# Another order for the first nine tiles of a fused attention and feed-forward kernel

## The chip, the cores and the metric

The kernel runs on one core of one Trainium2 chip. A core has TensorE (PE; its weight loads are PEld), VectorE (DVE), ScalarE (ACT), GpSimd (POOL) and the queues that issue transfers, SP's above all. Each engine works off its own instructions in the order in which they stand and waits on semaphores for the others. The metric is the device time of one execution in microseconds (us). Before the change it is 477.7 us, the median of three runs (477.04 to 478.3).

## The reference: what is computed

Chunked attention, then a feed-forward block with a SoLU and a layer norm:

```
scores = (q_c @ k_c^T) / 8          # batch 8, heads 8, 9 chunks of 64, head size 64
attn   = exp(scores - max); attn /= sum(attn) + 1e-9
x      = attn @ v_c                 # put together as 4608 tokens x 512
h      = x @ w_in                   # 512 x 1024
solu   = h * softmax(h)
ln     = (solu - mean) / sqrt(var + 1e-6) * g_ln
out    = ln @ w_out                 # 1024 x 512
```

q, k and v are float32. The weights reach the kernel as float64, as pairs of 32-bit words; the matrix products run as three products of two float32r halves each (high by high, high by low, low by high), so each weight matrix must first be cut into a high and a low part.

## The kernel before, in words

The 4608 tokens are 36 tiles of 128 tokens; a tile holds two chunks of each of the eight heads. From tile 5 on a loop runs one tile after another in a fixed pattern. Ahead of the loop stands a start in which four things run together: the weights are loaded and converted, attention is computed for tiles 0 to 7, the feed-forward products of tiles 0 to 4 are made, and the loads for the loop are begun. The order of that start is written out by hand as a string of words, START (lines 18 to 31). A word names a step and its tile or unit; where a word stands several times, each place issues the next piece of that step. Every engine keeps the order in which the words reach it. MOVED (lines 34 to 37) names the pieces that run on another engine than usual.

The steps that matter here:

- `n:i` two loads of q and k of tile i as they lie (256 KB each, one slot for even and one for odd tiles); `v:i` the load of v (256 KB); `P:x` a load of one unit of weights, 1 MB (unit 0 in two halves; units 0 to 3 are `w_in`, 4 to 7 `w_out`); `g` the load of g_ln; `q` some loads of the loop's q and k (`q_st`, `k_st`, 72 KB each). SP issues them all.
- A unit's conversion: `c:x` limits the upper words (line 188, tile `w_a`), then ACT scales them in place; `b:x` turns the lower words into bits (line 198, tile `w_b`); `C:x` joins both on DVE; `t:x` writes the high part on ACT; `d:x` the low part on DVE.
- Attention of tile i: `N` four PE transposes of q or of k and a copy out of PSUM to `qT` or `kT`; `S` scores on PE; `A` maximum and subtraction on DVE, then exponential on ACT; `B` sum, reciprocal and multiplication on DVE (the multiplication has both inputs in SBUF); `T` transposes on PE and four copies on ACT; `V` values on PE, then `x_h` on ACT and `x_l` on DVE.
- Feed-forward: `M:i` 24 products into `ph` on PE (tile 0 in four parts, part m with unit m); `X` maximum on DVE and exponential on ACT; `Y` a multiplication on DVE and an affine step on ACT or POOL; `R` the variance on ACT and POOL; `z` transposes of tiles 0 and 1 on PE with `z_h` on ACT and `z_l` on DVE; `Z` the same for tiles 2 and 3 by a DVE transpose and 16 transfers; `F` eight products into `po` on PE; `o` the scaling and the store on ACT; `w:n` n products of the identity that compute nothing.

`ph` has one buffer, except that tile 1 has one of its own: products of tile 2 and later wait until the multiplication of `Y` of the tile before in that buffer has read it. `w_a` and `w_b` have two buffers each. All transfers of SP and ACT share eight semaphores in turn, so each also waits for the landing of the one eight places ahead.

Every recorded operation has line 54 in the profile, that of the helper which keeps the order; rows are told apart by tiles.

Of the kernel before, what the change touches and what calls it, by code (L numbers as in the profile page):

```python
# [15 lines left out]


START = """
n:0 w:3 N:0:0 N:0:0 w:1 N:0:1 N:0:1 g w:1 S:0 A:0 G P:0 P:0 n:1 A:0 c:0 c:0 w:3 N:1:0 N:1:0 w:1
N:1:1 b:0 N:1:1 G P:1 w:1 S:1 B:0 v:0 C:0 A:1 t:0 T:0 T:0 c:1 c:1 w:4 V:0 V:0 P:2 b:1 c:2 n:2  # L20
d:0 P:3 A:1 n:3 w:6 N:2:0 w:1 N:2:1 C:1 V:0 B:1 t:1 c:2 T:1 N:2:0 b:2 N:2:1 T:1 d:1 S:2 n:4
M:0 M:0 C:2 t:2 c:3 c:3 v:1 A:2 A:2 b:3 d:2 C:3 N:3:0 N:3:1 N:3:1 M:0 N:3:0 S:3 N:4:0 B:2 N:4:1
t:3 N:4:0 A:3 P:5 d:3 c:5 N:4:1 A:3 T:2 T:2 S:4 V:1 M:0 P:4 n:5 B:3 T:3 V:1 V:1 M:1 X:0 X:0 T:3
A:4 A:4 b:4 v:2 N:5:1 c:4 n:6 P:7 c:5 N:5:0 c:4 Y:0 Y:0 n:7 N:5:1 V:2 b:5 v:3 B:4 N:5:0 V:2 b:7
C:4 z:0:1 P:6 v:5 N:6:0 X:1 v:4 C:5 N:6:0 S:5 Q:2 q:8 t:4 V:2 d:4 N:6:1 N:6:1 X:1 t:5 A:5 Y:1
M:2 z:0:1 z:0:1 X:2 A:5 R:0 z:0:0 z:0:0 q:8 N:7:1 q:8 c:6 S:6 Y:1 V:3 X:2 T:4 T:4 z:0:0 d:5 F
V:3 Y:2 Y:2 N:7:0 A:6 c:6 c:7 V:3 b:6 B:5 C:6 n:8 N:7:0 M:3 R:1 c:7 q:8 N:7:1 C:7 T:5 z:1:0 t:6
T:5 S:7 t:7 d:6 X:3 X:3 d:7 V:4 V:4 Y:3 Y:3 R:2 z:1:1 A:6 F F A:7 V:4 z:1:0 z:1:0 v:6 Z:2 A:7
M:4 F B:7 Z:3 o:0 V:5 z:1:1 z:1:1 B:6 F F v:7 X:4 N:8:0 X:4 U:6 U:7 V:5 Y:4 V:5 K:9 Y:4 N:8:0
R:4 R:3 N:8:1 N:8:1 o:1  # L30
"""


MOVED = """
N:0:0=dve N:8:0=dve N:8:1=dve Y:0=pool Y:1=pool Y:3=pool b:7=pool c:0=pool c:1=pool c:2=pool
c:3=pool c:4=pool c:5=pool c:6=pool c:7=pool
"""


# [23 lines left out]
def chunk_attention_then_solu_ffn(  # L63
# [12 lines left out]
    B, H, S, D = q.shape  # L76
    DM, FF = H * D, g_ln.shape[0]
    P = 128
# [3 lines left out]
    G = S // 32  # L82
# [24 lines left out]
    def po():  # L107
# [8 lines left out]
    moved = dict(w.split("=") for w in MOVED.split())  # L116
    order.on = False
    pe, dve, act, pool, sync = (
        order.engine(e)
        for e in (nc.tensor, nc.vector, nc.scalar, nc.gpsimd, nc.sync)  # L120
    )
# [89 lines left out]
    def paired(w):  # L211

        return w.rearrange("p (a x b) -> p a x b", x=2, b=P)
# [14 lines left out]
    def unit_low(x):  # L228
        kind, m = UNITS[x]
        a, top = scaled.pop(x), tops.pop(x)  # L230
        if kind == "in":
            dve.tensor_tensor(
                out=paired(wi_l[:, m, :]),
                in0=a.rearrange("p h (a b x) -> p (h a) x b", b=P, x=2),
                in1=top.bitcast(F32), op=ALU.subtract,
            )
            return
        for y in range(2):
            dve.scalar_tensor_tensor(
                out=wo_l[:, 2 * m + y, :], in0=a[:, y],  # L240
                scalar=g_sb[:, 2 * m + y:2 * m + y + 1], in1=top[:, y].bitcast(F32),
                op0=ALU.mult, op1=ALU.subtract,
            )


    QT, KT, V, QS, KS = {}, {}, {}, {}, {}
# [129 lines left out]
    def softmax_b(i):  # L376
        e = st[i, "e"]
        ssum = small.tile([P, H], F32, name="s_sum")
        dve.tensor_reduce(out=ssum, in_=ES[i % 2], axis=AX.X, op=ALU.add)
        rinv = small.tile([P, H], F32, name="s_rinv")  # L380
        dve.reciprocal(out=rinv, in_=ssum)
        a = st[i, "e"] = work.tile([P, H, CH], F32, name="s_e") if i < PE_TURNED else e
        dve.tensor_tensor(
            out=a, in0=e, in1=rinv.unsqueeze(2).to_broadcast([P, H, CH]), op=ALU.mult,
        )

# [330 lines left out]
    def warm(n):  # L717
# [8 lines left out]
        "P": load_pair, "n": load_natural,  # L726
        "v": load_v, "g": load_g, "Q": load_batch, "q": load_some,
        "G": scale_g, "N": turn_natural, "S": scores, "A": start_softmax, "B": softmax_b,
        "T": attn_transpose, "U": attn_turn, "V": start_values, "c": unit_scale,
        "b": unit_bits, "C": unit_join, "t": unit_high, "d": unit_low, "M": ffn_in, "X": solu_a, "Y": solu_b,  # L730
        "R": variance, "Z": z_turn, "z": z_half, "F": product, "o": store,
        "K": turn, "w": warm,
# [17 lines left out]
    for i in range(first, NT):  # L750
# [9 lines left out]
        if not odd:  # L760

            if i + 3 < NT:
                softmax_e(i + 3)
                softmax_b(i + 3)
                attn_turn(i + 3)
            if i + 1 < NT:
                x_high(i + 1)
# [27 lines left out]
        if odd:  # L795
            if i + 1 < NT:
                x_low(i + 1)
            if i + 3 < NT:
                softmax_b(i + 3)
                attn_turn(i + 3)  # L800
        else:
            for m in (i + 4, i + 5):
                if m < NT:
                    turn(m)
# [45 lines left out]
```

## Time and profile before

| what | us |
|---|---|
| median of three runs | 477.7 |
| the profiled execution | 477.95 |
| its span | 476.2 |
| PE busy | 465.6 (98%) |
| DVE busy | 374.3 (79%) |
| ACT busy | 256.5 (54%) |
| POOL busy | 147.7 (31%) |

A row of the timeline has the start, the duration, engine, line, operation, output and inputs, shape and count; in brackets stands how long the engine was idle before it and what ended that. A row of the windows has, for each engine, busy time and the number of instructions, then the granted TensorE clock, the share of the transfer engines and their rate. The granted clock is 1.00 throughout.

### The profile page before, as it was taken

To read this page: it belongs to the slowest core of one execution; us is meant where nothing else is said; L and a number is where in the kernel's file an instruction comes from. 1 tells how busy PE (TensorE), PEld (TensorE's weight loads), DVE (VectorE), ACT (ScalarE), POOL (GpSimd) and SP (SyncE) were. 2 spreads that over 40 slices of the span, in tenths; PEclk is the share of its full clock that TensorE was granted. 3 is DMA by queue.
4 is the path that set the end of the run, shared out by engine and by line. 5 is a ranking of instruction groups with operands and counts; after the bars stand their busy time and mean duration, and the time that the engine had idled before them with its cause. 6 is when DMAs were issued, how large, how long until landed. Compare 5 with 4: busy or idle time off the path is not lost.

```text
span 476.2 us, 11114 instructions
## 1 busy us (share of the span) xinstructions
PE 465.6 (98%) x4212; PEld 382.6 (80%) x4212; DVE 374.3 (79%) x520; ACT 256.5 (54%) x423; POOL 147.7 (31%) x298
## 2 busy tenths in 40 slices
PE   7899998999999999999999999999999999999997
PEld 5677786888888888888888888888888888888876
DVE  3999997798869887878787878797979797954441
ACT  2879982646444645454545455454555554545552
POOL 2212725150505050505050505032414141423330
PEclk9999999999999999999999999999999999999999
DMA  8999979758886878696358596949743435343221
GB/s 221 308 288 220 202 134 199 166 154 154 200 144 162 158 175 166 164 168 154 88 138 159 136 185 144 182 110 188 156 115 97 126 90 135 85 116 104 74 60 73
DMA packets 192924, 72.57 MB, mean 152 GB/s; under 512 B 177188, under 2 KB 177960, under 8 KB 191976
## 3 DMA queue, kind: packets, MB, share of 16 engines
q1 hardware_dynamic: 185768, 58.23, 55.4%
q0 software_dynamic: 6528, 12.86, 10.4%
q8 instruction: 33, 0.54, 0.5%
q10 hardware_dynamic: 576, 0.79, 0.5%
q14 instruction: 19, 0.16, 0.1%
HBM read 36.70 MB, written 9.44 MB: 97 GB/s over the span
## 4 chain that ended last, share of the span: by engine, by line
PE 85%; DMA 6%; SPq 3%; DVE 3%; ACT 1%; issue 1%; ACTq 0%
PE po L54 38%; PE ph L54 38%; PE tp L54 5%; PE sx L54 4%; SPq L54 3%; DMA nat<-in_k_dram 2%; DMA nat<-in_q_dram 2%; DMA z_t<-z_b 1%; DMA k_st<-in_k_dram 1%; DVE h_nmax L54 0%; DVE w_a L54 0%; DVE wo_l L54 0%; ACT attn_t L54 0%; ACT z L54 0%; ACT z_h L54 0%
## 5 line engine op out<-in xcount | busy, mean ns | idle before, releaser
L54 PE MATMUL ph<-wi_l,x_h 128*128 128x512 f32 x288 | 112.9, 392 | 1.9 <-DVE z L54 1.8
L54 PE MATMUL po<-wo_l,z_h 128*128 128x512 f32 (+1 forms) x288 | 113.3, 393 | 0.1
L54 ACT ACTIVATE z<-ph,h_nmax 128x1024 f32<-128x1024 f32 x36 | 40.2, 1117 | 134.6 <-DVE h_nmax L54 134.6
L54 PE MATMUL ph<-wi_h,x_h 128*128 128x512 f32 x288 | 112.1, 389 | 0.0
L54 PE MATMUL po<-wo_h,z_l 128*128 128x512 f32 (+1 forms) x288 | 111.9, 389 | 0.0
L54 PE MATMUL po<-wo_h,z_h 128*128 128x512 f32 (+1 forms) x288 | 111.4, 387 | 0.0
L54 POOL DMA_DIRECT2D z_t<-z_b x144 | 71.7, 505 | 28.7 <-DVE z_b L54 24.5
L54 PE MATMUL ph<-wi_h,x_l 128*128 128x512 f32 x288 | 78.1, 390 | 0.0
L54 POOL TENSOR_TENSOR u<-ssq,eps 128x1 f32<-128x1 f32 x36 | 7.1, 198 | 212.1 <-ACT sq L54 211.9
L54 DVE TENSOR_REDUCE h_nmax<-ph 128x1 f32<-128x1024 f32 x36 | 44.0, 1221 | 30.2 <-PE ph L54 30.2
L54 PEld LDWEIGHTS ph<-wi_l,x_h 128*128 128x128 f32 x288 | 54.1, 188 | 13.8 <-ACT x_h L54 2.2
L54 PEld LDWEIGHTS po<-wo_h,z_l 128*128 128x128 f32 x288 | 54.1, 188 | 12.1 <-DVE z_l L54 1.0
L54 PEld LDWEIGHTS po<-wo_l,z_h 128*128 128x128 f32 x288 | 54.1, 188 | 11.9 <-ACT z_h L54 0.5
L54 PEld LDWEIGHTS ph<-wi_h,x_l 128*128 128x128 f32 x288 | 53.9, 188 | 11.6 <-DVE x_l L54 0.4
L54 PEld LDWEIGHTS ph<-wi_h,x_h 128*128 128x128 f32 x288 | 54.1, 188 | 11.0
L54 PEld LDWEIGHTS po<-wo_h,z_h 128*128 128x128 f32 x288 | 54.1, 188 | 10.5
L54 DVE TENSOR_TENSOR z_l<-z_t,z_h 128x1024 fp32r<-128x1024 f32 (+1 forms) x37 | 42.0, 1136 | 25.3 <-ACT z_h L54 23.9
L54 DVE SCALAR_TENSOR_TENSOR z<-ph,z 128x1024 f32<-128x1024 f32 x36 | 43.9, 1219 | 13.3 <-ACT z L54 13.2
L54 ACT ACTIVATE z<-z,z_sum 128x1024 f32<-128x1024 f32 x33 | 38.1, 1154 | 23.0 <-DVE z L54 22.4
L54 DVE STREAM_TRANSPOSE z_b<-z 128x1024 f32<-128x1024 f32 x34 | 41.2, 1211 | 3.8 <-ACT z L54 3.1
L54 ACT CAST z_h<-z_t 128x1024 fp32r<-128x1024 f32 (+1 forms) x37 | 35.9, 970 | 8.6 <-PE po L54 6.5
L54 ACT ACTIVATE o_sb<-po,r 128x512 f32<-128x512 f32 (+1 forms) x36 | 24.2, 673 | 24.9 <-POOL r L54 18.6
(76 smaller groups left out, 598.6 us busy)
## 6 DMA issues: line engine op xcount, KB each, us to landing
out_dram<-o_sb SPq DMA_DIRECT2D x33, 256.0 KB, 2.5
v_sb<-in_v_dram SPq DMA_DIRECT2D x32, 256.0 KB, 4.4
z_t<-z_b POOLq DMA_DIRECT2D x128, 64.0 KB, 2.8
z_t<-z_b SPq DMA_DIRECT2D x128, 64.0 KB, 2.9
q_st<-in_q_dram SPq DMA_DIRECT2D x96, 72.0 KB, 3.1
k_st<-in_k_dram SPq DMA_DIRECT2D x96, 72.0 KB, 3.1
w_raw<-in_moe_w_out_dram SPq DMA_DIRECT2D x4, 1024.0 KB, 7.4
attn_t<-a_b POOLq DMA_DIRECT2D x60, 64.0 KB, 3.8
```

The lines of the kernel that those rows point to most:

```text
L54: ins = make(*args, **kwargs)
```

## The change

START is another sequence of the same words, and MOVED names another set of pieces. The words before and after are the same, but that two `w:3` have become `w:2` (19 of the empty products in place of 21). Two steps, `d` and `B`, get the possibility to run on POOL, which MOVED does not use.

```diff
 START = """
-n:0 w:3 N:0:0 N:0:0 w:1 N:0:1 N:0:1 g w:1 S:0 A:0 G P:0 P:0 n:1 A:0 c:0 c:0 w:3 N:1:0 N:1:0 w:1
+P:1 c:1 c:1 n:0 n:1 w:6 N:0:0 P:0 P:0 b:1 w:1 N:0:1 N:0:0 C:1 N:0:1 t:1 w:1 S:0 n:2 N:1:0 A:0
...
 MOVED = """
-N:0:0=dve N:8:0=dve N:8:1=dve Y:0=pool Y:1=pool Y:3=pool b:7=pool c:0=pool c:1=pool c:2=pool
-c:3=pool c:4=pool c:5=pool c:6=pool c:7=pool
+N:0:0=dve N:8:0=dve Y:2=pool Y:3=pool Y:4=pool b:2=pool b:5=pool c:0=pool c:2=pool c:3=pool
+c:4=pool c:5=pool c:6=pool c:7=pool
 """
...
         if kind == "in":
-            dve.tensor_tensor(
+            (pool if f"d:{x}" in moved else dve).tensor_tensor(
...
         a = st[i, "e"] = work.tile([P, H, CH], F32, name="s_e") if i < PE_TURNED else e
-        dve.tensor_tensor(
+        (pool if f"B:{i}" in moved else dve).tensor_tensor(
```

So c:1 and b:7 go from POOL to DVE, b:2 and b:5 from DVE to POOL, one copy of tile 8 from DVE to ACT, and of the affine steps Y:0 and Y:1 go from POOL to ACT, Y:2 and Y:4 from ACT to POOL.

**SP's queue at the start.** `nat` are the q and k of a tile, `w_raw` a unit of weights. Before:

```order
L54 DMA nat_95<-in_q_dram 128x8x64
L54 DMA nat_95<-in_k_dram 128x8x64
L54 DMA g_in_103<-in_moe_g_ln_dram 4x256
L54 DMA w_raw_151<-in_moe_w_in_dram 128x1024 x2
L54 DMA nat_95<-in_q_dram 128x8x64
L54 DMA nat_95<-in_k_dram 128x8x64
L54 DMA w_raw_183<-in_moe_w_in_dram 128x2048
L54 DMA v_sb_209<-in_v_dram 128x8x64
L54 DMA w_raw_252<-in_moe_w_in_dram 128x2048
```

With the change:

```order
L54 DMA w_raw_104<-in_moe_w_in_dram 128x2048
L54 DMA nat_95<-in_q_dram 128x8x64
L54 DMA nat_95<-in_k_dram 128x8x64
L54 DMA nat_95<-in_q_dram 128x8x64
L54 DMA nat_95<-in_k_dram 128x8x64
L54 DMA w_raw_127<-in_moe_w_in_dram 128x1024 x2
L54 DMA nat_95<-in_q_dram 128x8x64
L54 DMA nat_95<-in_k_dram 128x8x64
L54 DMA w_raw_201<-in_moe_w_in_dram 128x2048
L54 DMA g_in_103<-in_moe_g_ln_dram 4x256
L54 DMA v_sb_230<-in_v_dram 128x8x64
L54 DMA nat_95<-in_q_dram 128x8x64
```

Unit 1 now comes first, ahead of q and k of tiles 0 and 1; unit 0 follows those; v of tile 0 comes behind unit 2, and q and k of tile 3, which stood behind unit 3, stand ahead of it.

**PE ahead of tile 0's products**, from the values of tile 0 (`sx<-attn_t,v_sb`) to the first product into `ph` with weights. Before:

```order
L54 MATMUL sx_96<-attn_t_94,v_sb_209 64x64 x16
L54 MATMUL ph_266<-ident_79 128x256 x6
L54 MATMUL tp_275<-ident_79,nat_95 128x128 x4
L54 MATMUL ph_280<-ident_79 128x256
L54 MATMUL tp_282<-ident_79,nat_95 128x128 x4
L54 MATMUL tp_297<-ident_79,s_e_293 128x128 x4
L54 MATMUL sx_96<-kT_274,qT_273 64x64 x16
L54 MATMUL ph_331<-wi_l_91,x_h_249 128x512
```

With the change:

```order
L54 MATMUL sx_96<-attn_t_94,v_sb_230 64x64 x16
L54 MATMUL tp_314<-ident_79,nat_95 128x128 x4
L54 MATMUL ph_329<-ident_79 128x256
L54 MATMUL tp_331<-ident_79,nat_95 128x128 x4
L54 MATMUL tp_339<-ident_79,s_e_324 128x128 x4
L54 MATMUL sx_96<-kT_313,qT_312 64x64 x16
L54 MATMUL ph_376<-wi_l_91,x_h_309 128x512
```

The rows read alike, but the transposes of q and k and the scores are those of tile 2 before and of tile 3 now: one tile more is turned and scored ahead of tile 0's products.

**DVE around POOL's b:5.** `w_b_522` is written by b:5 on POOL, `w_a_454` belongs to unit 4 and `w_a_476` to unit 5. With the change DVE has:

```order
L54 TENSOR_SCALAR w_b_568<-w_raw_411 128x1024
L54 SCALAR_TENSOR_TENSOR z_570,z_sum_574<-ph_376,z_570 128x1024
L54 SCALAR_TENSOR_TENSOR w_a_454<-w_a_454,w_b_568 128x1024
L54 TENSOR_REDUCE s_nmax_577<-sx_96 128x8
L54 TENSOR_TENSOR e1_98<-sx_96,s_nmax_577 128x8x64
L54 TENSOR_TENSOR x_l_566<-sx_96,x_h_565 128x512
L54 TENSOR_REDUCE h_nmax_618<-ph_580 128x1
L54 TENSOR_TENSOR z_l_102<-tp_611,z_h_101 128x512
L54 SCALAR_TENSOR_TENSOR w_a_476<-w_a_476,w_b_522 128x1024
```

and POOL has:

```order
L54 TENSOR_SCALAR w_a_203<-w_raw_127 128x1024
L54 TENSOR_SCALAR w_a_261<-w_raw_201 128x1024
L54 TENSOR_SCALAR w_b_326<-w_raw_201 128x1024
L54 TENSOR_SCALAR w_a_383<-w_raw_273 128x1024
L54 TENSOR_SCALAR w_a_454<-w_raw_411 128x1024
L54 TENSOR_SCALAR w_a_476<-w_raw_435 128x1024
L54 TENSOR_SCALAR w_b_522<-w_raw_435 128x1024
```

In this order POOL does c:0, c:2, b:2, c:3, c:4, c:5, b:5. Before it did c:0, c:1, c:2, c:3, c:5, c:4, then an affine step and b:7. The multiplication of Y:0 and C:4 stand ahead of five DVE instructions that read PSUM, and C:5, which needs b:5, behind them.

More of the change, by code (lines that the diff above doesn't have):

```diff
@@ L18 @@
 START = """
-n:0 w:3 N:0:0 N:0:0 w:1 N:0:1 N:0:1 g w:1 S:0 A:0 G P:0 P:0 n:1 A:0 c:0 c:0 w:3 N:1:0 N:1:0 w:1
[L20 to L30, printed above, removed]
+P:1 c:1 c:1 n:0 n:1 w:6 N:0:0 P:0 P:0 b:1 w:1 N:0:1 N:0:0 C:1 N:0:1 t:1 w:1 S:0 n:2 N:1:0 A:0
@@ new lines @@
+N:1:0 N:1:1 N:1:1 w:2 S:1 d:1 A:0 P:2 c:0 c:0 A:1 w:2 N:2:0 N:2:0 w:1 N:2:1 b:0 g v:0 B:0 N:2:1
+w:1 S:2 C:0 n:3 A:1 c:2 T:0 t:0 T:0 P:3 n:4 A:2 G d:0 w:4 V:0 c:2 A:2 V:0 N:3:0 N:3:0 B:1 b:2 G
+w:1 N:3:1 v:1 N:3:1 T:1 V:0 T:1 S:3 B:2 C:2 A:3 t:2 M:0 c:3 M:0 n:5 c:3 v:2 N:4:0 b:3 N:4:0
+N:4:1 P:4 V:1 d:2 T:2 P:5 A:3 N:4:1 C:3 n:6 B:3 M:0 c:4 P:6 S:4 v:3 c:5 t:3 d:3 N:5:0 T:2 A:4
+V:1 V:1 N:5:1 N:5:1 N:5:0 M:0 P:7 A:4 X:0 B:4 b:5 T:3 T:3 S:5 V:2 V:2 b:4 X:0 c:4 Y:0 C:4 A:5
+M:1 Y:0 n:7 c:5 t:4 z:0:0 z:0:0 V:2 X:1 X:1 N:6:1 N:6:1 A:5 v:5 z:0:0 C:5 b:6 R:0 Q:2 q:8 d:4
@@ L31 @@
+M:2 Y:1 N:6:0 X:2 t:5 z:0:1 N:6:0 V:3 z:0:1 X:2 c:6 c:7 S:6 d:5 z:0:1 T:4 T:4 Y:2 V:3 v:4 F
+N:7:0 Y:2 Y:1 c:6 A:6 N:7:1 V:3 N:7:1 N:7:0 M:3 c:7 B:5 R:2 b:7 C:6 V:4 t:6 C:7 t:7 S:7 n:8 d:6
+z:1:0 T:5 d:7 F Z:2 T:5 X:3 V:4 V:4 F z:1:0 q:8 X:3 z:1:1 z:1:0 q:8 A:6 z:1:1 Y:3 V:5 V:5 A:7
+q:8 Y:3 v:6 z:1:1 F A:7 R:3 o:0 v:7 M:4 B:6 B:7 Z:3 X:4 U:6 U:7 F F X:4 R:1 Y:4 Y:4 N:8:1 V:5
+N:8:1 R:4 N:8:0 o:1 N:8:0 K:9
 """
 MOVED = """
-N:0:0=dve N:8:0=dve N:8:1=dve Y:0=pool Y:1=pool Y:3=pool b:7=pool c:0=pool c:1=pool c:2=pool
```

## The prediction

> **What bounds the kernel now.** I read the page first, then the busy time by stages, then PE's timeline, and followed PE's waits to what ended them.
>
> ```profile
> PE 465.6 (98%) x4212; PEld 382.6 (80%) x4212; DVE 374.3 (79%) x520; ACT 256.5 (54%) x423; POOL 147.7 (31%) x298
> PE   7899998999999999999999999999999999999997
> DVE  3999997798869887878787878797979797954441
> ```
>
> PE has hardly a gap. But part of it is empty products and waiting that counts as busy, so the stages say more:
>
> ```profile
> 0.00:23.36 23.36, 19.15 (x204) 14.58 (x205) 14.69 (x21) 13.14 (x20) 5.15 (x13) 1.00 0.93 264
> 23.36:34.21 10.85, 10.74 (x150) 8.40 (x145) 10.57 (x16) 9.20 (x16) 1.28 (x2) 1.00 1.17 290
> 34.21:82.15 47.94, 45.19 (x428) 36.20 (x426) 43.54 (x63) 34.20 (x64) 20.71 (x24) 1.00 0.92 191
> 82.15:200.00 117.85, 117.73 (x1104) 97.21 (x1105) 99.93 (x141) 62.33 (x102) 38.12 (x84) 1.00 0.77 163
> 200.00:400.00 200.00, 200.00 (x1822) 165.83 (x1821) 167.87 (x237) 104.19 (x168) 60.91 (x132) 1.00 0.63 142
> ```
>
> (columns: window, its length, then PE, PEld, DVE, ACT, POOL, clock, transfers' share, GB/s.) From 82.15 us on PE idles 0.12 us in 318: whatever PE gains by then reaches the end whole. 23.36 is where tile 0's first product starts, 34.21 that of tile 1, 82.15 that of tile 5, with which the loop begins. DVE is busy for 10.57 of 10.85 us and 43.54 of 47.94 in these stages, so it is a second chain as long as PE's. The transfers are full (0.93, 1.17) until 34 us: they set when the start can begin.
>
> ```profile
> 20.39 0.66 PE L54 MATMUL tp<-ident,nat 128*128 128x128 f32 x4 [0.65 <-DMA nat<-in_q_dram]
> 22.74 0.69 PE L54 MATMUL sx<-kT,qT 64*64 64x64 f32 x32 [0.24 <-ACT kT L54]
> 23.36 0.50 PE L54 MATMUL ph<-wi_l,x_h 128*128 128x512 f32 x1
> 40.55 1.06 PE L54 MATMUL tp<-ident,nat 128*128 128x128 f32 x8 [0.62 <-DMA nat<-in_k_dram]
> 41.55 0.69 PE L54 MATMUL sx<-attn_t,v_sb 64*64 64x64 f32 x32
> 82.15 0.47 PE L54 MATMUL ph<-wi_l,x_h 128*128 128x512 f32 x1 [1.84 <-DVE z L54]
> ```
>
> Tile 0's products start behind tile 2's scores, whose q landed at 20.39. Of the 2.75 us in which PE idles from 34.21 to 82.15 (47.94 - 45.19), 0.62 and 1.84 stand here. The longer one begins on ACT:
>
> ```profile
> 75.03 0.41 ACTq L630 DMA_DIRECT2D out_dram<-o_sb  x1
> 75.49 0.59 ACT L54 CAST z_h<-tp 128x512 fp32r<-128x512 f32 x1 [5.97 <-DMA k_st<-in_k_dram]
> 76.11 0.69 DVE L54 TENSOR_TENSOR z_l<-tp,z_h 128x512 fp32r<-128x512 f32 x1 [2.80 <-ACT z_h L54]
> 78.28 1.22 DVE L54 TENSOR_REDUCE h_nmax<-ph 128x1 f32<-128x1024 f32 x1
> 80.77 1.22 DVE L54 SCALAR_TENSOR_TENSOR z<-ph,z 128x1024 f32<-128x1024 f32 x1
> ```
>
> The store of tile 0 stood in ACT's queue for a `k_st` load of SP; behind it waited tile 1's `z_h`, behind that DVE, so tile 4's maximum came at 78.28 and its multiplication freed `ph` only at 82.
>
> **The change part by part.** Time is counted at the start of tile 5's products, 82.15 now; by then both kernels have done the same PE work.
>
> *When tile 0's products start.* POOL's c steps show when weights land:
>
> ```profile
> 9.60 1.62 POOL L54 TENSOR_SCALAR w_a<-w_raw 128x1024 f32<-128x1024 f32 x1 [8.17 <-DMA w_raw<-in_moe_w_in_dram]
> 14.17 1.14 POOL L54 TENSOR_SCALAR w_a<-w_raw 128x1024 f32<-128x1024 f32 x1 [2.95 <-DMA w_raw<-in_moe_w_in_dram]
> 17.98 1.54 POOL L54 TENSOR_SCALAR w_a<-w_raw 128x1024 f32<-128x1024 f32 x1 [2.68 <-DMA w_raw<-in_moe_w_in_dram]
> 24.14 1.13 POOL L54 TENSOR_SCALAR w_a<-w_raw 128x1024 f32<-128x1024 f32 x1 [4.62 <-DMA w_raw<-in_moe_w_in_dram]
> ```
>
> By 14.17 units 0 and 1 and q and k of tiles 0 and 1 are there, 3 MB; the change loads the same 3 MB first, so unit 0, now last of them, lands at 14.2 in place of 9.6, and unit 1 much earlier. From 14.17 to 24.14 came 2.75 MB, 3.63 us per MB (3.05 and 4.1 in its two pieces). The change needs unit 2 after 1.5 MB more: 19.6; v of tile 0 at 20.5; k of tile 3 after 2.25 MB: 22.3 (21.0 to 23.4). From there the copy to `kT` is held by ACT's queue, priced by these starts:
>
> ```profile
> 22.10 0.59 ACT L54 COPY kT<-tp 128x512 f32<-128x512 f32 x1 [0.43 <-PE tp L54]
> 22.58 1.54 ACT L54 COPY attn_t<-tp 64x256 f32<-64x256 f32 x4
> 24.14 1.14 ACT L54 CAST wi_h<-w_a 128x1024 fp32r<-128x1024 f32 x1
> 25.30 1.06 ACT L54 ACTIVATE w_a<-w_a 128x1024 f32<-128x1024 f32 x1
> 26.27 0.61 ACT L54 ACTIVATE e<-e 128x512 f32<-128x512 f32 x1
> ```
>
> A copy takes 0.48, four attention copies 1.56, a weight cast 1.16, a scaling 0.97, an exponential about 0.55. Unit 0 at 14.2, b:0 on DVE (0.6) and c:0 on POOL (1.1) one after the other: ACT can scale it at 16.1. Then follow scaling, five copies or `x_h`, two exponentials, one cast, the four copies and unit 2's scaling: 0.97 + 2.4 + 1.1 + 1.16 + 1.56 + 0.97 = 8.2, with 0.3 of short waits 24.6. Scores (0.62 by 22.74 to 23.36) and 0.2 of handing over: **25.4**, 2.0 later than 23.36. Bounds: 24.4 with the fastest loads, 27.9 with the slowest and c:0 held.
>
> *Work moved ahead of it.* Tile 3's eight transposes (40.55 to 41.55: 1.0) and its scores (0.62) leave what follows: -1.6.
>
> *The waits that go.* q and k of tile 6, which PE waited for at 40.55, now stand behind 1 MB less of weights; and tile 0's store comes after tile 3's variance on ACT, when tile 4's products are still running, so a late `k_st` no longer holds a `z_h` that PE needs. SP starts `q_st` earlier (units 4 to 7 and tiles 4 to 7 come in a row); the rows that price it, before, are
>
> ```profile
> 51.20 12.81 SPq L54 DMA_DIRECT2D q_st<-in_q_dram  x16
> 70.13 6.02 SPq L54 DMA_DIRECT2D k_st<-in_k_dram  x8
> ```
>
> 0.8 and 0.75 us per load. From about 47 the 27 loads and four others before the store's predecessor make 70; ACT is there at 70 and needs to be on with tile 4's exponential only at about 75: five us of cover, without which PE waits what exceeds it. -2.5 together; bounds 0 and -2.75.
>
> *Steps on other engines.*
>
> ```profile
> L54 ACT ACTIVATE z<-z,z_sum 128x1024 f32<-128x1024 f32 x33 | 38.1, 1154 | 23.0 <-DVE z L54 22.4
> L54 POOL TENSOR_SCALAR z<-z,z_sum 128x1024 f32<-128x1024 f32 x3 | 3.8, 1250 | 8.3 <-DVE z L54 8.2
> ```
>
> The four affine steps that change places are a draw: 1.15 us on ACT, 1.25 on POOL. c:1 on DVE costs what b:2 gives there, and b:7 what b:5 gives; tile 8's copy leaves DVE. DVE's load stays the same. But on POOL:
>
> ```profile
> 17.28 1.23 DVE L54 SCALAR_TENSOR_TENSOR w_a<-w_a,w_b 128x1024 uint32<-128x1024 uint32 x1
> 36.65 1.10 POOL L54 TENSOR_SCALAR w_a<-w_raw 128x1024 f32<-128x1024 f32 x1 [1.47 <-DMA w_raw<-in_moe_w_out_dram]
> 36.82 1.48 DVE L54 TENSOR_SCALAR w_b<-w_raw 128x1024 uint32<-128x1024 uint32 x1
> 39.36 0.68 DVE L54 TENSOR_SCALAR w_b<-w_raw 128x1024 uint32<-128x1024 uint32 x1
> 47.60 3.73 POOL L54 TENSOR_SCALAR w_b<-w_raw 128x1024 uint32<-128x1024 uint32 x1 [6.57 <-DVE s_nmax L54]
> ```
>
> A b takes 0.68 on DVE and 3.73 on POOL, and the two engines hold one another: DVE's b at 36.82 ended at 38.30, 0.55 after POOL's c that had begun before it (37.75), and POOL's c at 17.98 took 1.54, not 1.13, because it had to let C at 17.28 end (18.51). So POOL waits for a DVE instruction with two SBUF inputs; that DVE waits so for POOL no row shows. Where b:7 stands now, DVE reads PSUM all along and loses nothing. b:2 (from 20.7) has B:1's multiplication in its way, which tile 1's transposes ahead of tile 3's scores need: between 0 and 2.7 us of DVE, which is 0 to 1.3 on tile 0's start (26.7 at worst) and up to 0.7 at its last part, since C:2 needs b:2 anyway. I take 0.4 and 0.2, nearer the lower end, since no row shows the whole. b:5 comes after c:5; unit 5 lands 3.5 MB after unit 3 (25.5), at 38.1 with 3.63 per MB, 39.1 with 3.85 (24.14 to 36.65 for 3.25 MB). b:5 then starts about 40, as C:4 does. Behind C:4 DVE has five instructions that read PSUM, four of 512 columns and one of 1024, priced by
>
> ```profile
> 33.76 0.69 DVE L54 TENSOR_TENSOR x_l<-sx,x_h 128x512 fp32r<-128x512 f32 x1
> 34.37 1.21 DVE L54 TENSOR_REDUCE h_nmax<-ph 128x1 f32<-128x1024 f32 x1
> ```
>
> 4 x 0.69 + 1.21, less 0.08 of overlap at each of four seams (33.76 + 0.69 - 34.37): 3.65 us, just b:5's length. I take 0; bounds 0 and 3.7.
>
> *Sum.* +2.0 + 0.4 - 1.6 - 2.5 + 0.2 = -1.5. From the profiled execution's 477.95 (1.75 around its span stay): 476.45; that execution is 0.25 over the median of the runs, so against 477.7 **476.2**.
>
> The Trainium skill, in "SBUF — State Buffer", section "Who interferes with whom", says that a VectorE instruction in a two-port mode, or with two SBUF inputs against a GpSimd instruction that reads SBUF, and the GpSimd instruction block each other, the later one fully and until the first has ended. The rows at 17.28 and 36.82 agree; by that rule the second rival holds, at least.
>
> **The rivals.**
>
> 1. *b:5 gets ahead of C:4, and the change is slower.* If unit 5 lands before 38.9, b:5 starts before C:4 can, and C:4, with two SBUF inputs, stands until POOL is done: 2.5 to 3.7 us of DVE just where DVE feeds tile 0's multiplication, the `wo` halves and tile 2's `ph`. Neither chain has slack for it (43.54 of 47.94): 476.2 + 3.0 = 479.2. For it: the two starts lie within 1 us. Against: POOL also yields to whatever DVE began first.
> 2. *b:2 holds B:1's multiplication whole.* +3.3 - 1.6 - 2.5 + 0.7 = -0.1: 477.6. For it: c's and C's rows; against: none where DVE with two inputs waited.
> 3. *Neither holds, and the short waits go too.* +2.0 - 1.6 - 2.75 - 0.3 = -2.65: 475.05. The 0.3 are handovers like the 0.24 at 22.74. For it: the stretch behind C:4 fits.
>
> **How the numbers follow.** Forecast 0.36 (its own range 475.2 to 477.2), rival 1 0.17, rival 2 0.21, rival 3 0.26. A difference of 0.3%, 1.4 us, is about what a measurement of this kernel can tell from none. Faster by more: 0.22 of the forecast, 0.25 of rival 3, 0.03 of rival 2, together 0.50. Slower by more: 0.15 of rival 1, 0.05 of rival 2 with late loads, 0.01: 0.21. The rest, 0.29, is within. Low end: rival 3 with the fastest loads (1.0 less) 474.05, rounded to 473.9; high end: rival 1 and a little, 479.4.
>
> **What would show it.** Tile 0's first product at 25.4 to 26.2; unit 0's c step at 14.2; tile 5's first product at 80.6, with no wait of 1.8 us before it and ACT without 6 us before `z_h`; POOL's b:2 and b:5 at 3.7 each and, beside them, DVE's multiplication of B:1 and C:4 at their usual 0.69 and 1.22 (longer by what POOL has left, where a rival holds). From tile 5 on the same 394 us. I am wrong if the opening loads land later than 14.2 and 22.3 by over a microsecond, or if DVE, not PE, makes tile 5 late.

## The result and the profile after

The changed kernel takes 482.42 us, the median of six runs (480.65 to 484.22), the kernel before beside it 477.37 (474.99 to 479.15): ratio 1.0112, 95% interval 1.0082 to 1.0142. It is slower, where faster was forecast, and 482.42 lies above the range. Chips differ by a few tenths of a per cent (the kernel before had medians of 475.4 to 477.4 on them), so experiments below are given as ratios to the kernel before on the same chip.

The page of the changed kernel (busy time, PE's slices, the granted clock's slices, the costliest group):

```profile
PE 467.1 (97%) x4208; PEld 383.0 (80%) x4208; DVE 373.6 (78%) x519; ACT 256.7 (53%) x424; POOL 149.8 (31%) x298
PE   8889999799999999999999999999999999999997
PEclk9999999899999999999999999999999999999999
L54 PE MATMUL po<-wo_l,z_h 128*128 128x512 f32 (+1 forms) x288 | 114.0, 396 | 2.5 <-ACT z_h L54 2.5
```

The totals hardly differ from those before (PE 465.6). But at the eighth slice, 84 to 96 us, PE has a 7 and the clock an 8, and a group that had no gap to speak of now waited 2.5 us for `z_h`. The windows of the changed kernel place it (columns as before: window, length, PE, PEld, DVE, ACT, POOL, clock, transfers' share, GB/s; 25.28 is tile 0's first product, 80.67 tile 5's):

```profile
25.28:80.67 55.39, 53.40 (x535) 43.40 (x529) 52.84 (x74) 43.95 (x82) 19.42 (x23) 1.00 0.97 211
80.67:86.30 5.63, 5.63 (x27) 4.41 (x25) 2.48 (x5) 1.07 (x3) 4.24 (x8) 1.00 0.96 207
86.30:91.85 5.55, 2.42 (x129) 2.17 (x128) 0.82 (x2) 2.32 (x4) 0.74 (x2) 0.99 1.09 177
91.85:95.50 3.65, 3.61 (x8) 2.45 (x9) 3.62 (x5) 1.20 (x2) 0.00 (x0) 0.55 0.26 44
95.50:200.00 104.50, 103.90 (x926) 85.50 (x925) 88.25 (x126) 55.84 (x90) 32.60 (x71) 1.00 0.72 153
```

Tile 5 starts at 80.67, 1.5 us earlier than in the profile before, and the forecast said 80.6. Between these two profiles everything is lost behind it (beside other executions of the kernel before the opening loses too, as is shown below): from tile 5's first product to the end of the span it is 480.5 - 80.67 = 399.8 us where it had been 476.2 - 82.15 = 394.05. Of these 5.8 us, 3.1 are idle time in 86.30 to 91.85, 0.6 idle time later, and 1.7 the clock, which the trace has at one half for 3.41 us from 91.73 on; 0.4 stay unplaced. PE's own rows:

```profile
87.78 0.63 PE L54 MATMUL sx<-attn_t,v_sb 64*64 64x64 f32 x27 [0.69 <-DMA attn_t<-a_b]
88.72 0.68 PE L54 MATMUL tp<-attn_t,v_sb 64*64 64x64 f32 x31
91.85 0.80 PE L54 MATMUL po<-wo_l,z_h 128*128 128x512 f32 x1 [2.45 <-ACT z_h L54]
```

and ACT's, with the one step of POOL that they wait for:

```profile
85.85 1.06 ACT L54 ACTIVATE sq<-z 128x1024 bf16<-128x1024 f32 x1 [4.56 <-POOL z L54]
86.91 0.67 ACT L54 ACTIVATE o_sb<-po,r 128x512 f32<-128x512 f32 x1
89.84 0.34 ACTq L630 DMA_DIRECT2D out_dram<-o_sb  x1
90.76 1.04 ACT L54 CAST z_h<-z_t 128x1024 fp32r<-128x1024 f32 x1 [3.18 <-DMA q_st<-in_q_dram]
```

```profile
84.69 1.12 POOL L54 TENSOR_SCALAR z<-z,z_sum 128x1024 f32<-128x1024 f32 x1
```

Two holds stand one behind the other on ACT. First, its `sq` of tile 4 (the squares for the variance) waits for tile 4's affine step, which the change put on POOL behind eight `z_t` and four `attn_t` transfers that POOL issues. Then tile 1's `o_sb` is written at 87.58, but its store goes only at 89.84, and tile 2's `z_h`, which PE needs, stands behind the store. The store stands for a semaphore: SP's and ACT's transfers use eight in turn, and the one eight places ahead of this store is now the second `q_st` load of the loop's first pass. By the trace's semaphore events that load landed at 89.76, 0.08 before the store went. In the kernel before the place was that of a `v_sb` load, landed at 87.31, and the store went at 87.39. The hand-written order settles what each engine does after what, but not how ACT's stores count in between SP's loads: by the semaphores, two of those `q_st` loads counted ahead of the store before, now nine.

### The profile page after: what moved, and what is told of

Same layout as the page of the kernel before. It is cut to its first block, busy times and chain, and to the rows that moved or that the text cites. A ratio compares the mean times of both kernels' runs of the same rounds, so it can differ in the third digit from the quotient of the medians.

```text
span 480.5 us, 11103 instructions
## 1 busy us (share of the span) xinstructions
PE 467.1 (97%) x4208; PEld 383.0 (80%) x4208; DVE 373.6 (78%) x519; ACT 256.7 (53%) x424; POOL 149.8 (31%) x298
## 4 chain that ended last, share of the span: by engine, by line
PE 71%; SPq 15%; DMA 8%; DVE 3%; issue 2%; ACT 1%; ACTq 0%; DVEq 0%
PE po L54 33%; PE ph L54 31%; SPq L54 15%; DMA v_sb<-in_v_dram 4%; PE sx L54 4%; PE tp L54 3%; DMA nat<-in_q_dram 2%; DMA nat<-in_k_dram 1%; DMA q_st<-in_q_dram 1%; DVE z_l L54 1%; DVE h_nmax L54 0%; DVE e L54 0%; ACT z_h L54 0%; DVE z L54 0%; DVE s_nmax L54 0%
## 5 line engine op out<-in xcount | busy, mean ns | idle before, releaser
L54 ACT ACTIVATE z<-z,z_sum 128x1024 f32<-128x1024 f32 x33 | 38.1, 1153 | 22.7 <-DVE z L54 22.2
L54 ACT ACTIVATE sq<-z 128x1024 bf16<-128x1024 f32 x36 | 37.6, 1043 | 4.6 <-POOL z L54 4.6
```

The lines of the kernel that those rows point to most:

```text
L54: ins = make(*args, **kwargs)
```

## The experiments

### Which of the two holds it is

Theory S is the store's semaphore, theory P the affine step on POOL. The first edit puts the affine step back:

```diff
-N:0:0=dve N:8:0=dve Y:2=pool Y:3=pool Y:4=pool b:2=pool b:5=pool c:0=pool c:2=pool c:3=pool
+N:0:0=dve N:8:0=dve Y:2=pool Y:3=pool b:2=pool b:5=pool c:0=pool c:2=pool c:3=pool
```

> The changed kernel with tile 4's affine step (z<-z,z_sum) back on ACT, nothing else. Theory S (the store's wait): in the changed kernel ACT stands for 2.26 us, from 87.58 to 89.84, at tile 1's store, which takes over the completion semaphore of tile 8's second q_st load (landed 89.77); z_h of tile 2 stands behind the store on ACT. The affine step is not in it, so z_h stays at about 90.8, PE idles about 2.4 us before tile 2's first po<-wo_l,z_h, and the time stays at 481 to 483. Theory P (the affine step on POOL): ACT's sq waited 4.56 us until 85.85 for POOL's affine step; on ACT it would be done at about 81.5, z_h would start near 87 when z_t has landed, PE would not idle there, and the time would be 476 to 478.5.

Measured: 480.88 us, ratio 1.0106 (1.0091 to 1.0121): no gain. ACT in this run:

```profile
85.30 0.69 ACT L54 ACTIVATE o_sb<-po,r 128x512 f32<-128x512 f32 x1 [1.28 <-POOL r L54]
90.25 0.34 ACTq L630 DMA_DIRECT2D out_dram<-o_sb  x1
91.17 1.04 ACT L54 CAST z_h<-z_t 128x1024 fp32r<-128x1024 f32 x1 [5.18 <-DMA q_st<-in_q_dram]
```

`o_sb` is there over a microsecond earlier, and the store just waits longer, until the load (landed 90.18). Theory P by itself is refuted. The store's place among the transfers is also the same as with the step on POOL, so in the changed kernel the new order alone is enough to put it there.

The second edit moves only that step in the kernel before:

```diff
-N:0:0=dve N:8:0=dve N:8:1=dve Y:0=pool Y:1=pool Y:3=pool b:7=pool c:0=pool c:1=pool c:2=pool
+N:0:0=dve N:8:0=dve N:8:1=dve Y:0=pool Y:1=pool Y:3=pool Y:4=pool b:7=pool c:0=pool c:1=pool c:2=pool
```

> The kernel before with tile 4's affine step on POOL, nothing else. It also hands tile 1's store the completion semaphore of tile 8's second q_st load, where the kernel before had that of a v_sb load (landed 87.31). Theory S: that q_st load lands between 90 and 93.6 here (93.60 in the kernel before), so the store goes then, z_h 0.9 us later at 91 to 94.5 (88.31 before), PE idles 1.5 to 5 us at its end, the clock drops behind it, and the time is 480 to 485. Theory P: POOL's step ends at about 84.4 and not 83.2, so the store's data is ready at 87.4 instead of 86.2, the store goes when it went, and the time is 477 to 478.5.

Measured: 480.27 us, ratio 1.0085 (1.0057 to 1.0112). One affine step, a draw by its own duration, costs the kernel before 4 us, since it shifts the count:

```profile
85.03 0.67 ACT L54 ACTIVATE o_sb<-po,r 128x512 f32<-128x512 f32 x1
88.76 0.34 ACTq L630 DMA_DIRECT2D out_dram<-o_sb  x1
89.67 1.04 ACT L54 CAST z_h<-z_t 128x1024 fp32r<-128x1024 f32 x1 [3.97 <-DMA q_st<-in_q_dram]
```

The load landed at 88.69, earlier than I had thought; PE idled 2.46 us and the clock fell as in the changed kernel.

The third edit takes the store off ACT, with all steps on their new engines:

```diff
-            store_rest()
+            store_rest(nc.gpsimd if i == 1 else None)
...
-    def store_rest():
+    def store_rest(engine=None):
...
-            (sync if order.on and len(stores) == 1 else nc.scalar).dma_start(to, of)
+            (engine or (sync if order.on and len(stores) == 1 else nc.scalar)).dma_start(to, of)
```

> The changed kernel with tile 1's store issued by POOL instead of ACT, so that ACT has no store ahead of tile 2's z_h. All five steps stay on their new engines, the affine step on POOL too. Theory S: z_h starts at about 87.6 (z_t has landed at 86.72, o_sb is written at 87.58) and not 90.76, tile 2's first product follows the turns at about 89.4 without the 2.45 us of idle time, the clock stays at 1.00 there (0.55 in 91.85 to 95.5, which cost about 1.6 us), and the time falls by about 4.1, to 477.5 to 479. Theory P: nothing falls by more than 0.5; 481.5 to 483.

Measured: 477.51 us, ratio 1.0050 (1.0024 to 1.0076). That is 3.6 us less than the 481.1 which 1.0112 makes of this chip's 475.78. PE has no gap over 0.2 us behind tile 5, and `z_h` follows `o_sb` without a pause:

```profile
85.92 0.67 ACT L54 ACTIVATE o_sb<-po,r 128x512 f32<-128x512 f32 x1
86.49 1.03 ACT L54 CAST z_h<-z_t 128x1024 fp32r<-128x1024 f32 x1
```

From tile 5 on it takes 475.3 - 80.40 = 394.9 us again. So the store on ACT is the loss behind tile 5. `sq` still waits 3.84 us for POOL here, and without a store behind it that costs PE nothing. What is left, 0.5%, is mostly the opening (below).

### Is it the semaphore, and are the two holds independent

The next kernel leaves the instructions of PE, DVE, ACT and POOL alone and only has SP issue five `q_st` loads a pass later, so that another transfer stands eight places ahead of the store:

```diff
-        load_some(LOADS[1])
+        load_some(LOADS[1] + {first: -5, first + 1: 5}.get(i, 0))
```

> The changed kernel with five of the q_st loads that SP issues in the loop's first pass issued in the second; PE, DVE, ACT and POOL do exactly the same in the same order, the store of tile 1 on ACT too. But the transfers count round differently, and the store takes over the semaphore of the second attn_t transfer (landed 86.51 in the changed kernel) and not that of the second q_st load (89.77). Theory S: the store goes when o_sb is written, at about 87.6, z_h starts 0.9 later at 88.5, tile 2's first product waits 0 to 0.3 us, the clock stays: like the run with the store on POOL, ratio to the kernel before 1.003 to 1.007, about 477.5. Rival: ACT's issue of a transfer waits for SP's queue or for the transfer engines as such, which are as busy as before in that stretch; then z_h stays at 90.8 and the ratio at 1.011 to 1.013.

Measured: 482.43 us, ratio 1.0132 (1.009 to 1.0175). The time is that of the rival, but the trace is that of theory S in the place that it speaks of:

```profile
87.39 0.67 ACT L54 ACTIVATE o_sb<-po,r 128x512 f32<-128x512 f32 x1
88.09 0.34 ACTq L630 DMA_DIRECT2D out_dram<-o_sb  x1
89.00 1.04 ACT L54 CAST z_h<-z_t 128x1024 fp32r<-128x1024 f32 x1 [0.95 <-DMA q_st<-in_q_dram]
```

```profile
90.10 0.50 PE L54 MATMUL po<-wo_l,z_h 128*128 128x512 f32 x1 [1.45 <-ACT z_h L54]
91.36 0.50 PE L54 MATMUL po<-wo_h,z_l 128*128 128x512 f32 x1 [0.53 <-DVE z_l L54]
```

The store goes the moment `o_sb` is written, while the transfer engines are still full (share 1.05 from 86.0 to 88.1, 1.26 there in the changed kernel). SP has just issued the last of its four loads here, so this run alone does not speak against a wait for SP's queue. The other stores do: in all eight profiles of the two kernels and their variants in which this store stood with `o_sb` written, it went 0.075 or 0.076 us after the landing of the transfer eight places ahead (of `v_sb`, `q_st` or `attn_t`, landed between 83.40 and 92.34), and SP had further loads to issue each time. What I had missed is that the first hold alone is late enough: `sq` waited 5.1 us for POOL, and from the store's issue to the start of `z_h` ACT takes 0.91 us (88.09 to 89.00; 89.84 to 90.76 in the changed kernel). PE still idled 1.45 + 0.53 us and the clock still fell. So both edits together:

```diff
-N:0:0=dve N:8:0=dve Y:2=pool Y:3=pool Y:4=pool b:2=pool b:5=pool c:0=pool c:2=pool c:3=pool
+N:0:0=dve N:8:0=dve Y:2=pool Y:3=pool b:2=pool b:5=pool c:0=pool c:2=pool c:3=pool
...
-        load_some(LOADS[1])
+        load_some(LOADS[1] + {first: -5, first + 1: 5}.get(i, 0))
```

> The changed kernel with both: the five q_st loads issued a pass later, so that tile 1's store takes over an attn_t transfer's semaphore, and tile 4's affine step back on ACT. Each alone left a PE gap before tile 2's first product (1.45 us with the loads alone, where ACT wrote o_sb only at 87.39 because its sq had waited 5.1 us for POOL's affine step; 2.13 with the affine step alone, where o_sb was there at 85.30 and the store waited until 90.25). Theory of two holds in a row on ACT: with both gone o_sb is written at 85.3 to 86, the store goes at 86.0 to 86.6, z_h starts 0.9 later at 87 to 87.5, PE waits 0 to 0.3 us, the clock stays at 1.00, and the ratio to the kernel before is 1.003 to 1.007 (1.005 with the store on POOL), plus up to 0.002 for the loads that come a pass later. Rival: the loss lies elsewhere in the stretch (the loop's first pass as a whole), the gap stays above 1 us and the ratio at 1.010 to 1.013.

Measured: 479.57 us, ratio 1.0068 (1.0047 to 1.0089). ACT, then the two PE gaps that the whole loop still has, and DVE's wait behind the first:

```profile
83.54 0.69 ACT L54 ACTIVATE o_sb<-po,r 128x512 f32<-128x512 f32 x1 [0.81 <-POOL r L54]
85.02 0.34 ACTq L630 DMA_DIRECT2D out_dram<-o_sb  x1
85.93 1.04 ACT L54 CAST z_h<-z_t 128x1024 fp32r<-128x1024 f32 x1 [1.71 <-DMA attn_t<-a_b]
```

```profile
138.83 0.62 PE L54 MATMUL tp<-kT,qT 64*64 64x64 f32 x26 [3.06 <-DVE kT L54]
141.33 0.50 PE L54 MATMUL po<-wo_h,z_l 128*128 128x512 f32 x1 [0.69 <-DVE z_l L54]
```

```profile
138.33 0.45 DVE L54 STREAM_TRANSPOSE kT<-k_st 128x256 f32<-128x256 f32 x1 [8.80 <-DMA k_st<-in_k_dram]
```

The store now waits for the second `attn_t` transfer (landed 84.94, store at 85.02), `z_h` comes almost five microseconds earlier, the gap before tile 2's first product is gone and the clock stays. The 3.7 us of gaps at 138 to 141 are the price of my loads a pass later, which the whole kernel would have to be arranged for. With each hold alone removed, and the store still on ACT, the gap stayed (2.13 and 1.45 us); with both gone it went. That is why neither edit alone moved the time.

### What the clock does after a gap

Empty products fill the gap in the changed kernel, with `z_h` left as late as it is.

```diff
+        if i == 2 and part == 0:
+            m = ident.unsqueeze(1).to_broadcast([P, 2, P])
+            for _ in range(8):
+                pe.matmul(
+                    st[i, "o"][0][:, :2 * P].rearrange("p (x m) -> p x m", x=2),
+                    ident, m, start=True, stop=True,
+                )
```

> The changed kernel with eight empty 128x256 products (about 0.27 us each, 2.1 us together) on PE ahead of tile 2's first product, in the 2.45 us in which PE idles. z_h still comes when it came. If the reduced clock in 91.85 to 95.5 follows from the idle time, the first rows of tile 2 take 0.39 us instead of 0.63 to 0.80 and the time falls by about 1.6 us, to 480.3 to 481.3. If the clock falls for another reason (the work of the stretch as a whole), nothing changes: 482 to 483.

Measured: 482.3 us, ratio 1.0132 (1.0108 to 1.0156): no gain in time. In its profile the clock did stay at 1.00 where it had fallen: 90 to 95 us in the changed kernel, and the same window here, in which PE runs the empty products:

```profile
90.00:95.00 5.00, 3.11 (x7) 2.01 (x8) 3.13 (x4) 1.82 (x2) 0.00 (x0) 0.67 0.52 108
```

```profile
90.00:95.00 5.00, 5.00 (x142) 4.60 (x143) 0.56 (x1) 1.47 (x2) 0.67 (x2) 1.00 1.07 188
95.00:100.00 5.00, 5.00 (x24) 4.13 (x23) 4.97 (x8) 2.98 (x5) 0.00 (x0) 1.00 0.12 20
```

But the products took 3.72 us, not 2.1, so they ended 1 us behind `z_h`, and in this execution the opening was 3.6 us late: PE idled 1.37 and 1.45 us at 29 to 32, and there too the clock fell to one half for 3.41 us. From tile 5 to the end it took 397.2 us, 2.6 less than the changed kernel's 399.8. Tile 2's first product stands 11.2 us behind tile 5's in both, so the 2.6 come after it: 1.7 are the clock, 0.6 the idle time that the changed kernel has at 143. That fits a clock that falls as a consequence of idle time, at a price of 1.7 us, but this run does not show it: it is one profile, the clock also stayed at 1.00 behind an empty gap of 2.13 us in the run of the first edit, and the run's time shows no gain. By the mean clock of each execution (one fall makes 0.996, two 0.992) eight of ten executions of the changed kernel had a fall, three of four with the empty products, one of twelve in the two runs with tile 1's store on POOL, whose opening is nearly the same, and one of the 59 of the kernel before whose clock is on record.

Over all profiles a fall ahead of the kernel's tail always came behind a gap: the clock stood at 0.5 for 3.41 us behind gaps of 2.45, 2.46, 2.17, 2.74, 2.00, 4.32, 1.45 + 0.53 and 1.37 + 1.45 us, and not behind 3.06, 2.13, 1.84 and 1.62. The Trainium skill, in "TensorE: Matmul & The Clock Gate", Part 1, says that the clock is set by the activity in a free-running window of about 3.4 us. The length agrees, and so do the places: in all fourteen profiles the times between two changes of the clock are whole multiples of 3.413 us (85.33 is 25 of them, 27.31 is 8). Counted along that grid, the window just ahead of a fall held 1.8 to 2.7 us of idle time, once all of it, while the gap of 3.06 is cut into 1.6 and 1.4, which would be why 2.17 lowered the clock and 3.06 did not. But where the section speaks of an idle window, 1.8 us in it were enough here, and the 2.0 us that the gap of 2.13 left in one window were not, so idle time alone does not decide, and what else does is not shown.

### The opening, and what the profile before was worth

Both kernels unaltered, once more, on one chip:

> The changed kernel once more, unaltered, for a pair of profiles from one chip together with the next run, and to see how far its opening moves from execution to execution. Tile 5's first product stood at 80.67 (the changed kernel), 80.40, 81.59 and 84.24 (three altered ones with the same opening). Theory: the opening is 80.4 to 81.6 where the clock stays at 1.00 and 2 to 3 us later where PE's gaps at 29 to 32 lower it; behind it the store's wait of tile 1 costs 4 to 5 us in every execution. Time 480.5 to 483. Rival: the loss behind tile 5 belonged to that one execution; then the time is below 479.

> The kernel before once more, unaltered. Its profile has PE waiting 1.84 us at 82.15, behind tile 0's store, which waits on ACT for a k_st load; the kernel before with one affine step moved has 0.24 us there, at 80.43. Theory V: that wait is a matter of the execution, and this profile has tile 5's first product at 80.3 to 81.3 with less than 1 us of it, so the change's opening gains 0 to 0.5 us and not 1.4 in a typical execution. Rival: the wait is the rule, 82 again, and the other profile was the exception.

Measured: the changed kernel 480.75 us, ratio 1.0129 (1.0097 to 1.0162), so the loss is no accident of one execution. The kernel before 475.81, ratio to itself 1.0010 (0.9996 to 1.0024); its profile, of the fastest of the eight executions (474.50 us), has tile 5's first product much earlier than the one I had worked from:

```profile
22.62 0.50 PE L54 MATMUL ph<-wi_l,x_h 128*128 128x512 f32 x1
78.91 0.47 PE L54 MATMUL ph<-wi_l,x_h 128*128 128x512 f32 x1 [0.17 <-DVE z L54]
```

```profile
71.83 0.37 ACTq L630 DMA_DIRECT2D out_dram<-o_sb  x1
72.25 0.59 ACT L54 CAST z_h<-tp 128x512 fp32r<-128x512 f32 x1 [3.98 <-DMA k_st<-in_k_dram]
```

```profile
22.62:78.91 56.29, 55.55 (x575) 44.67 (x569) 53.86 (x78) 43.17 (x80) 21.91 (x25) 1.00 1.08 216
```

The store of tile 0 still waits for a `k_st` load, but 3.98 us and not 5.97, and of PE's 1.84 us at 82.15 there are 0.17 left. The kernel before had 0.24 there in the run with one affine step moved. The wait that the change was to save is mostly that one profile's.

> The kernel before with the stores of tiles 0 and 1 issued by POOL instead of ACT. Theory S: ACT's z_h of tile 1 no longer stands for a k_st load (5.97 us in the profile before), so tile 5's products start at 80.2 to 80.5 in every execution; tile 2's z_h starts when z_t has landed, 0.3 to 1 us earlier than now, which PE does not need. Against the kernel before 0 to -1.8 us: 474.5 to 475.8. If POOL's issuing (0.64 us each, behind it POOL's z_t transfers) delays z_t, it is up to 0.6 us slower instead.

The edit is that of the store on POOL, for `i < 2`. Measured: 474.99 us, ratio 0.9996 (0.9985 to 1.0007). Without either store on ACT, tile 5 starts at 79.26 with no wait before it, as good as the 78.91 with them. Since that ratio is one of medians, it holds for the typical execution: the stores cost the kernel before nothing that can be measured. It is also no improvement.

With these profiles the opening can be added up (first products of tiles 0 and 5; PE's idle and busy time between them):

| kernel | tile 0 | tile 5 | idle | busy |
|---|---|---|---|---|
| before, the profile of the prediction | 23.36 | 82.15 | 2.87 | 55.92 |
| before, once more | 22.62 | 78.91 | 0.74 | 55.55 |
| before, stores of tiles 0 and 1 on POOL | 22.37 | 79.26 | 1.51 | 55.38 |
| changed | 25.28 | 80.67 | 1.99 | 53.40 |
| changed, once more | 25.11 | 80.82 | 2.05 | 53.66 |
| changed, store of tile 1 on POOL | 25.13 | 80.40 | 1.84 | 53.43 |

Tile 0 starts about 2.7 us later than it did in the two later profiles of the kernel before, 2.0 us of PE's work are done ahead of it, and PE idles 0.3 to 1.3 us more: the opening loses 1 to 2 us where the sum had a gain of 1.5. With the 0.3 to 1.1 us behind tile 5 (394.1 and 394.9 in the two runs with the store on POOL, beside 472.7 - 78.91 = 393.8) that adds up to the 0.5%, 2.0 to 2.4 us, that is left without the store; these are sums over single profiles. Where PE idles, in the changed kernel:

```profile
30.19 0.63 PE L54 MATMUL tp<-ident,nat 128*128 128x128 f32 x4 [1.41 <-DMA nat<-in_k_dram]
31.11 0.69 PE L54 MATMUL sx<-attn_t,v_sb 64*64 64x64 f32 x32 [0.29 <-DMA v_sb<-in_v_dram]
```

The next edit loads these ahead of unit 3 (with tile 1's store on POOL):

```diff
-w:1 S:2 C:0 n:3 A:1 c:2 T:0 t:0 T:0 P:3 n:4 A:2 G d:0 w:4 V:0 c:2 A:2 V:0 N:3:0 N:3:0 B:1 b:2 G
-w:1 N:3:1 v:1 N:3:1 T:1 V:0 T:1 S:3 B:2 C:2 A:3 t:2 M:0 c:3 M:0 n:5 c:3 v:2 N:4:0 b:3 N:4:0
+w:1 S:2 C:0 n:3 A:1 c:2 T:0 t:0 T:0 n:4 v:1 P:3 A:2 G d:0 w:4 V:0 c:2 A:2 V:0 N:3:0 N:3:0 B:1 b:2 G
+w:1 N:3:1 N:3:1 T:1 V:0 T:1 S:3 B:2 C:2 A:3 t:2 M:0 c:3 M:0 n:5 c:3 v:2 N:4:0 b:3 N:4:0
```

> The changed kernel with tile 1's store on POOL, and q and k of tile 4 and v of tile 1 loaded ahead of unit 3 instead of behind it. In the changed kernel PE idles 1.1 to 1.6 us at 29 to 30 for k of tile 4 and 0.2 to 1.6 at 31 for v of tile 1. Theory O: these waits, which the prediction's sum left out, are half of what the opening loses against the kernel before; without them tile 5's products start 1 us earlier, at 79.4 to 79.8, and the ratio falls from 1.005 to 1.002 to 1.004. Rival: unit 3 lands 2.5 us later, at about 29, and the wait only moves to its conversion and to tile 0's last part; ratio 1.005 to 1.01.

Measured: 480.45 us, ratio 1.0092 (1.0059 to 1.0126), the rival's. The two waits are gone, and one of 4.32 us has come: ACT's scaling of unit 3 now waits for the later unit, and tile 4's copy of q stands behind it on ACT.

```profile
33.97 1.12 PE L54 MATMUL tp<-ident,s_e 128*128 128x128 f32 x4 [4.32 <-ACT qT L54]
```

So in this place the loads compete: what brings `nat` and v forward makes unit 3 late (it landed at 30.55, 26.83 in the changed kernel). This other order is worse; that the order of the change is the best one was not tested.

### The engines

> The changed kernel with tile 1's store on POOL, and the two weight steps b:2 and b:5 back on DVE (0.68 us each there, 4.1 each on POOL). By the prediction POOL's b:2 costs 0.4 us on tile 0's start and 0.2 later, b:5 nothing: against the run with the store alone, 477.5, that is 476.9. If DVE's load is what limits this stretch (DVE is busy 38.8 of the 40.5 us before tile 5), DVE's 1.4 us more cost up to 1.4: 478.9. If POOL's long steps slow DVE or the loads more than the rows show, 475 to 476.

(Tile 1's store on POOL, and `b:2=pool b:5=pool` taken out of MOVED.) Measured: 477.40 us, ratio 1.0047 (1.0033 to 1.0061), beside 1.0050 with both steps on POOL; tile 5's first product at 80.87 beside 80.40. The two steps change nothing that can be measured; the 0.6 us that the prediction has for b:2 is too small to be told from none here.

> The changed order of steps with all steps on the engines of the kernel before, and tile 1's store on POOL: the new order alone. Against the run with the store on POOL and the new engines (ratio 1.005). By the prediction the engines are a draw but for b:2's 0.6 us: ratio 1.003 to 1.006, tile 5's products at 80 to 81. If the new engines are what the opening loses by, the ratio falls to 1.000 to 1.002; if the order needs them, it rises above 1.008.

(START of the change, MOVED of the kernel before, tile 1's store on POOL.) Measured: 483.12 us, ratio 1.0156 (1.0112 to 1.0201). The new order with the old engines is worse than the change, by two waits that the profile names, one for an affine step on POOL and one of `C:7` for `b:7` on POOL:

```profile
46.06 0.66 PE L54 MATMUL tp<-ident,z 128*128 128x128 f32 x4 [2.00 <-POOL z L54]
```

```profile
68.81 1.22 DVE L54 SCALAR_TENSOR_TENSOR w_a<-w_a,w_b 128x1024 uint32<-128x1024 uint32 x1 [5.12 <-POOL w_b L54]
```

The second makes PE wait 2.74 us for `wo_l`, and behind each the clock fell. So some of the moves to other engines belong to the new order. That of tile 4's affine step is one that hurts (with five loads a pass later, 1.0132 with it and 1.0068 without); the others were not tried one by one.

## Why the prediction was wrong, by its own steps

**What bounds the kernel.** "Whatever PE gains by then reaches the end whole" was the step that failed first, with "from tile 5 on the same 394 us" in the list of what would show it: it was 399.8, and 394.9 once tile 1's store was off ACT. The second is the term of -2.5, below. That PE idled 0.12 us in 318 said that nothing was waited for behind tile 5, not by how much. The trace before had the answer (ACT, then PE):

```profile
87.39 0.34 ACTq L630 DMA_DIRECT2D out_dram<-o_sb  x1
88.31 1.05 ACT L54 CAST z_h<-z_t 128x1024 fp32r<-128x1024 f32 x1 [2.08 <-DMA attn_t<-a_b]
```

```profile
90.19 0.50 PE L54 MATMUL po<-wo_l,z_h 128*128 128x512 f32 x1
```

Tile 1's store went at 87.39, tile 2's `z_h` behind it was done at 89.36, and PE used it at 90.19, right behind other work, so that less than a microsecond of slack lay behind a store that waited for a semaphore. I had named the rule of the eight semaphores and followed tile 0's store by it, but never looked up which transfer stands eight places ahead of tile 1's store in the changed order.

**Four affine steps are a draw.** By their durations they are, 1.15 and 1.25 us. But Y:4 on POOL stands behind twelve transfer issues, and the whole chain `sq`, `o_sb`, store, `z_h` behind it. In the kernel before, this step alone also shifts the store's place among the transfers and costs 4 us; in the changed kernel the place is the shifted one with the step and without it. This term was put at 0 without the cover that it needs being named.

**Tile 0's start.** 25.4 forecast, 25.28 and 25.1 measured. But the term was +2.0 against 23.36, and in later profiles of the kernel before and its variants tile 0 starts at 22.3 to 22.6, so it is nearer +2.7. These landings were right within 0.7 us: unit 0's c at 13.49 (14.2 forecast), k of tile 3 at 22.66 (22.3), unit 2 at 19.44 (19.6), unit 5 at 39.37 (38.1 to 39.1). Unit 3 came at 26.83, not at 25.5; by the prediction's own rate, 1 MB behind k of tile 3, it would have been 25.9. The work moved ahead was 2.0 to 2.5 us of PE, where I had 1.6.

**The waits that go, -2.5.** Both went, and ACT had no 6 us ahead of `z_h`. But 1.84 of the 2.5 were in the one profile before and are 0.17 to 0.24 in others, and the sum left out the gaps that came, 1.4 to 2.8 us together at 28 to 32 in the runs with the opening of the change. Tile 5 at 80.67 against 80.6 was right only beside that profile, which is luck; beside the 78.91 and 79.26 of later ones it is a loss.

**Steps on other engines.** b:2 and b:5 are harmless as far as can be measured; they took 4.12 and 4.05, not 3.73. For b:2 the changed kernel has, on POOL and then on DVE:

```profile
21.39 4.12 POOL L54 TENSOR_SCALAR w_b<-w_raw 128x1024 uint32<-128x1024 uint32 x1
```

```profile
21.20 0.69 DVE L54 TENSOR_TENSOR s_e<-e,s_rinv 128x512 f32<-128x512 f32 x1
25.13 0.69 DVE L54 TENSOR_TENSOR s_e<-e,s_rinv 128x512 f32<-128x512 f32 x1
```

The multiplication of B:1, which rival 2 saw behind b:2, began 0.19 us before it, so the rival's case did not come up. That of B:2 began at 25.13, inside b:2 (until 25.51), and took its usual 0.69. Of rival 1 the condition came, b:5 before C:4, but not the cost:

```profile
39.52 1.43 POOL L54 TENSOR_SCALAR w_a<-w_raw 128x1024 f32<-128x1024 f32 x1 [1.49 <-DMA w_raw<-in_moe_w_out_dram]
41.03 4.05 POOL L54 TENSOR_SCALAR w_b<-w_raw 128x1024 uint32<-128x1024 uint32 x1
```

```profile
39.90 1.61 DVE L54 TENSOR_SCALAR w_b<-w_raw 128x1024 uint32<-128x1024 uint32 x1
42.56 1.22 DVE L54 SCALAR_TENSOR_TENSOR w_a<-w_a,w_b 128x1024 uint32<-128x1024 uint32 x1
```

C:4, with two SBUF inputs, began 1.5 us after b:5 and took its usual 1.22 beside it; b:5 was 0.3 longer than b:7 had been on POOL, by what is not shown. DVE's own b at 39.90 did wait, as in the rows of the prediction, until POOL's c had ended (39.52 + 1.43 = 40.95, then its 0.56). So the full block that the Trainium skill states for two SBUF inputs ("SBUF — State Buffer", "Who interferes with whom") was not seen for C:4 and for B:2's multiplication.

**The range.** Its upper end, 479.4, was rival 1. No rival stood behind tile 5, though the words that tile 1's store hangs on (`R:1`, `Y:4`, `R:4`, `o:1`) stand at the hand-over to the loop, `R:1` new there and `Y:4` on another engine, so the range could not hold the result.

## What to carry to other kernels

In this kernel a store that a compute engine issues held that engine until the transfer ahead of it on its semaphore had landed. So when an order changes, look up for every such store which transfer that is now and when it lands, and what is queued behind the store; or issue it from an engine with nothing urgent behind it. An engine that never waits in a profile shows no slack: read how late its inputs could be, from when each was ready and when it was used. And where one wait carries the forecast, see first whether other executions of the same kernel have it.

## What was not expected of the hardware

A gap of PE can cost more than its length: behind some two microseconds of idle time in a short stretch the granted clock often stood at one half for 3.41 us, which is 1.7 us of work more. A gap of 3.06 us and one of 2.13 left it alone, and the two profiles of the kernel before, with gaps up to 1.84, have no fall before their tail. One and the same opening differed by over 3 us between executions. Before, tile 5 stood at 78.91 and 82.15: tile 0 started 0.7 us apart, and 2.1 of the rest are idle time, behind loads that landed sooner or later. With the opening of the change it stood at 80.40 and 84.24 (two of the altered kernels): 1.6 us more idle time and the clock's fall behind it.
